# Linear attention beside a gated feed-forward block: x's statistics moved to the head of each iteration, and another order of loads where the token half changes

## The chip, the cores and the metric

The kernel runs on one core of a Trainium2 chip. A core has five engines, each with its own queue of instructions: PE (TensorE, matmuls), DVE (VectorE), ACT (ScalarE), POOL (GpSimd) and SP (SyncE), which here issues every DMA. The metric is the time on the device in microseconds (us), as the median of several runs. A trace comes from one more execution under the hardware profiler.

## What is computed

Everything is fp32. x has 2048 tokens of 576 values. It is normalized, and the result goes into two branches whose product is added to x:

```python
xn = layernorm(x)
q, k, v = split(xn @ wqkv)                    # 32 heads of 18
pq, pk  = phi(q), phi(k)                      # phi(t) = (t + 1 if t > 0 else exp(t)) + 1e-6
kv, z   = per head: pk^T v, sum of pk
s       = ((pq kv) / (pq z + 1e-6)) @ wo
g       = silu(gelu(xn @ w1 + b1) @ w2 + b2)  # w1: 576 x 4608, w2: 4608 x 576
out     = x + s * g
```

## The kernel before

A value is kept as two fp32r parts, high and low; a product is three matmuls (high by high, high by low, low by high). A "split" is a cast on ACT (high) and a subtraction on DVE (low).

**First stage** (the loop `for t in range(NT)`, 16 tiles of 128 tokens). Iteration t makes k and v of tile t and prepares later tiles. In program order: load of x of tile t+3; `project` for k (PE, 28 matmuls into pk); `transpose_x(t+1)` (five PE transposes of xn into pt, cast to xh on ACT, low part xl and a last block of xh on DVE); splits of w2's operand sums (`w2_hi`, `w2_lo`, tag w2o) and, in iterations 2 to 6, of w1's last rows (`we_hi`, `we_lo`, tag w1h); `layernorm(t+2)`; `phi` of k; `state(t-1)` (PE); `project` for v; `normalize_x(t+2)` (ACT writes xn); then on POOL the sums `w2_sum` and, in iterations 1 to 5, `we_sums`, and the addition of phi(k) to zacc; and the stores of what was split. `layernorm(t)` is two bn_stats, an aggregate and an add on DVE, the power -1/2 on POOL (`mv[:, 3:4]`), and for t of 2 and more a one-column product on DVE (L187, mean times -1/sqrt) that ACT uses as the bias in `normalize_x`. The instructions of each engine stand in the order of the program (`in_order`) until the end of the second stage. SP's DMAs are one queue; a DMA waits for the eighth before it.

The second stage makes q and the attention output. **The third stage** is the feed-forward block, 18 steps: the 9 chunks of w1 and w2 (512 hidden columns each), first over tokens 1024 to 2047 (half 0), then over the others (half 1). A step (base = 28 times its number) has an up part of two w1 tiles, n = 2 step and 2 step + 1, each seven products in the order UP = (1, 6, 7, 5, 2, 3, 4) of a Winograd scheme (L962, PSUM tiles a, b, zy, e), and a down part of seven products in the order ORDER = (1, 2, 7, 4, 5, 3, 6) (L1092, pm), whose results DVE adds to macc. PE, DVE, ACT and POOL follow program order; the extra work is put at places of the step by `add(base + place, function)`; places 0 to 13 follow the up products, 14 to 27 the down products. In half 0 the operands of w1 and w2 are made and stored; in half 1 they are loaded: `load_we` (we), `W1Loaded` (tiles a, c, d, and for odd n the tile e with operand 6 of both), `W2.load`.

The last step of half 0 is step 8 (NC is 9). In it the operands of x for half 1 are loaded over those of half 0: seven parts of 1 MiB (h0, l0, s2, h1, l1, s1, s4: high, low and sums of x's blocks, `load_x_part`) and, for each of the seven products, a last block of 128 rows (`load_rest`, two DMAs of 128 KB; into tiles rx for products 5, 2, 3, 4). `X_PARTS` says from where and into which place (`x_hi(b)` is xh of block b, `x_lo(b)` xl). In half 0 product 1 and 2 read xh2 and xl2, product 6 reads xh0, 5 xl1, 3 xl0, 7 and 4 xh3 and xl3. In half 1 product 1 and 2 read h0 and l0, 6 s2, 7 and 4 h1 and l1, 5 s1, 3 s4.

Of the kernel before, what the change touches and what calls it, by code (L numbers as in the profile page):

```python
# [42 lines left out]
def linear_attention_gated_ffn(ctx, tc, x, wqkv, wo, w1, w1e, b1, w2, b2, out):  # L43
# [36 lines left out]
    def bank2(name):  # L80
        return psum.tile([P, 2, 512], F32, tag="pp", name=name)
# [91 lines left out]
    def layernorm(t):  # L173
        st = t1.tile([P, 2, 6], F32, tag="st", name=f"st{t}")
        nc.vector.bn_stats(st[:, 0, :], xraw[t][:, :HD])
        nc.vector.bn_stats(st[:, 1, :], xraw[t][:, HD:])
        mv = t1.tile([P, 4], F32, tag="mv", name=f"mv{t}")
        nc.vector.bn_aggr(mv[:, 0:2], st)
        nc.vector.tensor_scalar_add(mv[:, 2:3], mv[:, 1:2], 1e-5)
        nc.gpsimd.tensor_tensor(mv[:, 3:4], mv[:, 2:3], nhalf, op=ALU.pow)  # L180
        xn[t] = t1.tile([P, 640], F32, tag="xn", name=f"xn{t}")
        if t < 2:
            for dst, src in norm_parts(t):
                nc.vector.tensor_scalar(dst, src, mv[:, 0:1], mv[:, 3:4], op0=SUB, op1=MUL)
        else:

            nc.vector.scalar_tensor_tensor(  # L187
                mv[:, 2:3], mv[:, 0:1], -1.0, mv[:, 3:4], op0=MUL, op1=MUL
            )
            stats[t] = mv  # L190

    def norm_parts(t):
        return (xn[t][:, :D], xraw[t]), (xn[t][:, D:], xraw[t][:, 512:])

    def normalize_x(t):
        mv = stats.pop(t)
        for dst, src in norm_parts(t):
            nc.scalar.activation(dst, src, AF.Identity, scale=mv[:, 3:4], bias=mv[:, 2:3])

# [230 lines left out]
    for t in range(NT):  # L430
        if t + 3 < NT:
            load_x(t + 3)
        if t == 1:
            we_load(0), we_load(1)
        pk = bank2(f"pk{t}")
        project(t, wk_h, wk_l, pk)
        if t == 0:
            for k in range(KT):
                split_w(raw_v[k], k, wv_h, wv_l, nc.vector)
        if t + 1 < NT:  # L440
            if t + 1 in (8, 12):
                x_block((t + 1) // 4)
            transpose_x(t + 1)
        for j in W2_SUMS.get(t - 1, ()):
            w2_hi(j)
        for j in W2_SUMS.get(t - 1, ()):
            w2_lo(j)
        if 2 <= t < 2 + WG:
            we_hi(t - 2), we_lo(t - 2)
        if t + 2 < NT:  # L450
            layernorm(t + 2)
        k_t, _ = phi(t1, pk, f"k{t}")
        if pend is not None:
            state(*pend)
        pv = bank2(f"pv{t}")
        project(t, wv_h, wv_l, pv)
        v_t = t1.tile([P, D], F32, tag="v", name=f"v{t}")
        nc.scalar.copy(as2(v_t), pv[:, :, :HD])
        if t + 2 < NT:
            normalize_x(t + 2)  # L460
        if t == 0:
            nc.gpsimd.memset(zacc, 0.0)
        for j in W2_SUMS.get(t, ()):
            w2_sum(j)
        if 1 <= t < 1 + WG:
            we_sums(t - 1)
        nc.gpsimd.tensor_tensor(zacc, zacc, k_t, op=ADD)
        for k in WQ_SPLITS.get(t, ()):
            split_w(raw_q[k], k, wq_h, wq_l, nc.gpsimd if k == 0 else nc.vector)
        for k in WQ_LOADS.get(t, ()):  # L470
            raw_q[k] = load_w_raw(0, k)
        for j in W2_SUMS.get(t - 1, ()):
            w2_store(j)
        if 2 <= t < 2 + WG:
            we_store(t - 2)
            if t < WG:
                we_load(t)
        for c in W2_LOADS.get(t, ()):
            w2_load(c)
        if t == KT + 2:  # L480
            make_mask()
            nc.gpsimd.memset(kvz, 0.0)
        pend = (t, k_t, v_t)
        if t in (4, 8):
            b = t // 4 - 1
            if b == 0:
                nc.sync.dma_start(x_dram[:, 0:4], xh[0][:, :4].bitcast(F32))
                nc.sync.dma_start(x_dram[:, 4:8], xl[0].bitcast(F32))
            else:
                nc.sync.dma_start(x_dram[:, 10:12], xh[1][:, 2:4].bitcast(F32))  # L490
                nc.sync.dma_start(x_dram[:, 14:16], xl[1][:, 2:].bitcast(F32))
# [164 lines left out]
        k, tag, bufs = (4, "w6", 1) if i == 6 else (8, "wa", 5)  # L656
        return w1p.tile([P, k, P], F32R, tag=tag, name=f"w{i}_{n}", bufs=bufs)

    we_sb = {}

    def load_we(n):

# [9 lines left out]
    class W1:  # L672
# [39 lines left out]
        def product(self, i):  # L712

            r = we_sb[self.n][:, WE_AT[i]]
            if i == 6:
                t = self.tiles[6]
                return t[:, :2], t[:, 2:], r
            key, k = {1: "a0", 2: "a1", 7: "c0", 3: "c1", 5: "d0", 4: "d1"}[i]
            t, k = self.tiles[key], 2 * int(k)
            return t[:, k : k + 2], t[:, 4 + k : 6 + k], r  # L720

    class W1Loaded(W1):


        def __init__(self, n):
            self.n, self.tiles = n, {}
            for i in ("a", "c", "d"):
                if n % 2 and i == "a":
                    t = w1_tile("e", n)
                    for k in range(2):  # L730
                        six = t[:, 4 * k : 4 * k + 4]
                        nc.sync.dma_start(six.bitcast(F32), w1_dram[(n - 1 + k) % NP, 6])
                        (w1t[n - 1] if k == 0 else self).tiles[6] = six
                if i == "c":
                    t = w1r.tile([P, 8, P], F32R, tag="stw", name=f"wc_{n}")
                else:
                    t = w1_tile(i, n)
                self.tiles[i] = t
                nc.sync.dma_start(t.bitcast(F32), w1_dram[n % NP, i])

    def spill(n):
        z = xsum[0]
# [493 lines left out]
    def x_operands(h0, l0, h1, l1, s1, s2, s4, rs):  # L1236
# [5 lines left out]
            3: (s4[:, A], s4[:, B]),  # L1242
        }.items()}

    X_PARTS = {
        "h0": (0, x_hi, 2, 1), "l0": (4, x_lo, 2, None), "s2": (16, x_hi, 0, 6),
        "h1": (8, x_hi, 3, 7), "l1": (12, x_lo, 3, None), "s1": (20, x_lo, 1, None),
        "s4": (24, x_lo, 0, None),
    }
    x_new = {}  # L1250

    def load_x_part(k):
# [64 lines left out]
    for step in range(n_chunks):  # L1317
# [4 lines left out]
        if half == 0:  # L1322
            plan_w1(add, w1t[2 * step + 1], base, **P1)
            add(base + 2, w2t[step].sum7)
            for i, at in PW2.items():
                add(base + at, w2t[step].hi, i)
                add(base + at + 1, w2t[step].lo, i)
            if step == 0:
                for i, at in W2_SUMS_FIRST.items():
                    add(at, w2t[0].load, i)  # L1330
        if not plain:
            add(base + 7, load_we, 2 * step + 2)
            add(base + 14, load_we, 2 * step + 3)
        if half == 0 and c < NC - 1:
            add(base + 0, make, W1, w1t, 2 * step + 2)
            add(base + 4, make, W1, w1t, 2 * step + 3)
            add(base + 1, lambda n=2 * step + 2, base=base: plan_w1(add, w1t[n], base, **P0))
            make(W2, w2t, step + 1)
            add(base + 22, w2t[step + 1].load_raw)
            for i, at in W2_SUMS_NEXT.items():  # L1340
                add(base + at, lambda i=i, n=step + 1: w2t[n].load(i))
        elif not plain:
            add(base + (14 if half == 0 else 7), make, W1Loaded, w1t, 2 * step + 2)
            add(base + 14, make, W1Loaded, w1t, 2 * step + 3)
            if step + 2 < n_chunks:
                make(W2, w2t, step + 1)
                for i, at in W2_NEXT.items():
                    add(base + at, lambda i=i, n=step + 1: w2t[n].load(i))
            else:
                make(W2, w2t, step + 1)  # L1350
                add(base + 7, w2t[step + 1].load_raw)
        if not plain:
            if half == 0 and c == NC - 1:
                for k, at in {"h0": 13, "l0": 13, "s2": 13, "h1": 15, "l1": 15, "s1": 15, "s4": 15}.items():
                    add(base + at, load_x_part, k)
                add(base + 15, lambda: x_new.update(rs=load_rests(0, (5, 2, 3, 4))))
                add(base + 25, silu_first, C11)
                for k in range(2):
                    add(base + 26 + k, combine, C12, nc.vector, slice(2 * k, 2 * k + 2))
                    add(base + 26 + k, combine, C21, nc.gpsimd, slice(2 * k, 2 * k + 2))  # L1360
            for what in ("S", "hi", "lo"):
                for (i, pr), at in PH[what].items():
                    add(base + at, getattr(h, what), i, pr)
        else:
            for f in range(CF):
                w2t[step].plain(f)
                add(base + (1, 2, 3, 8)[f], w2t[step].hi, ("p", f))
                add(base + (2, 3, 8, 9)[f], w2t[step].lo, ("p", f))
# [86 lines left out]
```

## Time and profile before

| what | us |
|---|---|
| median of 3 runs (lowest to highest) | 1121.29 (1120.52 to 1122.15) |
| the profiled execution | 1125.7 |
| its span, from first to last instruction | 1124.0 |
| PE busy in it | 1104.1 |
| DVE, ACT, POOL busy | 815.1, 455.9, 449.5 |

A row of a timeline is start, length, engine, line, operation, what is written from what is read, and in brackets the idle time of the engine before it and what ended that. A row of waits is who waited for whom: us in total, times, longest. A row of windows gives busy time and count by engine, then the clock that PE was granted (1.00 is full), the busy share of the DMA engines and GB/s. The chain is the work that ended last, followed back.

### The profile page before, as it was taken

The page shows a single profiled execution, that of the slowest core. Times are in us where ns is not written, and L with a number is a line of the kernel's source. Part 1 is how long each engine was busy: PE and PEld are TensorE (multiplying, and loading weights), DVE is VectorE, ACT ScalarE, POOL GpSimd, SP SyncE. Part 2 cuts the span into 40 slices and gives each one's busy share as a digit, 9 for nine tenths or more (in the row PEclk, how much of TensorE's full clock was granted, in tenths as well). Part 3 has the DMA queues.
Part 4 walks back from the last instruction along what each step waited for, and adds up shares of the span by engine and source line. Part 5 has one row for each costly group of instructions (what it writes and reads, how often), then busy time and mean ns, then how long its engine had stood idle before and what let it go on. Part 6 is the DMA issues. An engine that isn't in the chain of part 4 may idle for free.

```text
span 1124.0 us, 18604 instructions
## 1 busy us (share of the span) xinstructions
PE 1104.1 (98%) x6972; PEld 1019.6 (91%) x6972; DVE 815.1 (73%) x1159; ACT 455.9 (41%) x771; POOL 449.5 (40%) x392
## 2 busy tenths in 40 slices
PE   8989999999999999999999999899999999999997
PEld 8989998999998988989989889698998998989987
DVE  6776657989687787878877868376585674765856
ACT  4544444333544354454443534424233242232342
POOL 4666543333353452453534524225133242341340
PEclk9999999999999999999999999899999999999999
DMA  8698732364879559577595599996877786766552
GB/s 313 245 390 303 256 140 51 125 246 159 273 270 326 207 196 333 186 263 261 182 326 208 197 312 327 320 324 198 287 226 218 211 236 210 245 217 207 140 159 104
DMA packets 84969, 264.03 MB, mean 235 GB/s; under 512 B 10381, under 2 KB 20877, under 8 KB 81295
## 3 DMA queue, kind: packets, MB, share of 16 engines
q1 hardware_dynamic: 84879, 262.85, 68.8%
q8 instruction: 55, 0.90, 0.3%
q14 instruction: 35, 0.29, 0.1%
HBM read 166.69 MB, written 94.18 MB: 232 GB/s over the span
## 4 chain that ended last, share of the span: by engine, by line
PE 90%; DMA 5%; DVE 2%; issue 1%; SPq 0%; ACT 0%; POOL 0%; DVEq 0%; ACTq 0%; POOLq 0%
PE pm L1092 32%; PE a L962 10%; PE e L962 10%; PE zy L962 10%; PE pq L226 5%; PE b L962 5%; PE ps_s L625 5%; PE pv L226 4%; PE pk L226 4%; PE pd L1212 2%; DMA rx<-rq_dram 1%; DMA w1u<-w1e 1%; PE ps_kva L263 1%; DMA we<-we_dram 1%; DMA w__7651<-op 1%
## 5 line engine op out<-in xcount | busy, mean ns | idle before, releaser
L1099 DVE TENSOR_TENSOR macc<-pm,macc 128x576 f32<-128x576 f32 x218 | 164.4, 754 | 58.8 <-PE pm L1092 57.0
L649 ACT CAST h_h<-g 128x512 fp32r<-128x512 f32 x204 | 120.9, 620 | 135.9 <-PE pm L1092 134.7
L652 DVE TENSOR_TENSOR h_l<-g,h_h 128x512 fp32r<-128x512 f32 x204 | 164.8, 815 | 0.0
L1061 POOL TENSOR_TENSOR mid<-g 128x512 f32<-128x512 f32 x34 | 43.9, 1292 | 134.3 <-ACT g L970 134.3
L1055 POOL TENSOR_TENSOR g<-g 128x512 f32<-128x512 f32 x34 | 55.1, 1620 | 57.7 <-DVE h_l L652 56.4
L970 ACT ACTIVATE g<-b,b1c 128x512 f32<-128x512 f32 x36 | 24.8, 690 | 122.9 <-DVE b L988 122.9
L979 ACT COPY mid<-a 128x512 f32<-128x512 f32 x36 | 21.1, 587 | 117.4 <-PE a L962 117.4
L693 POOL TENSOR_TENSOR w1raw<-w1raw 128x256 f32<-128x256 f32 x18 | 16.9, 938 | 124.1 <-DVE wa L709 124.1
L982 DVE TENSOR_TENSOR mid<-b,mid 128x512 f32<-128x512 f32 x36 | 24.7, 687 | 44.9 <-PE b L962 43.2
L1058 POOL TENSOR_TENSOR g<-g 128x512 f32<-128x512 f32 x34 | 55.4, 1630 | 2.7
L1187 POOL TENSOR_TENSOR fin1l<-fin1h,fin1l 128x288 f32<-128x288 f32 x8 | 6.5, 807 | 121.9 <-DMA fin1l<-s_dram 56.6
L962 PE MATMUL a<-h0r,wa 128*128 128x512 f32 x144 | 51.5, 398 | 0.0
L988 DVE TENSOR_TENSOR b<-e,mid 128x512 f32<-128x512 f32 x36 | 25.2, 700 | 36.0 <-PE e L962 36.0
L962 PE MATMUL a<-xh,wa 128*128 128x512 f32 x144 | 50.6, 391 | 0.0
L1052 POOL TENSOR_TENSOR g<-g 128x512 f32<-128x512 f32 x34 | 46.7, 1373 | 2.7
L652 DVE TENSOR_TENSOR h_l<-mid,h_h 128x512 fp32r<-128x512 f32 x34 | 45.8, 1348 | 1.2
L590 POOL TENSOR_TENSOR pbuf<-phiq,den 128x576 f32<-128x576 f32 x16 | 20.4, 1276 | 63.6 <-DVE den L589 44.8
L985 DVE TENSOR_TENSOR mid<-zy,mid 128x512 f32<-128x512 f32 x36 | 24.9, 692 | 26.3 <-PE zy L962 26.3
L995 DVE TENSOR_TENSOR e<-e,mid 128x512 f32<-128x512 f32 x36 | 24.9, 691 | 22.8 <-PE e L962 22.7
L295 POOL TENSOR_TENSOR w2r<-w2r 128x576 f32<-128x576 f32 x27 | 41.0, 1526 | 0.7
L970 ACT ACTIVATE g<-e,b1c 128x512 f32<-128x512 f32 x36 | 24.9, 691 | 34.0 <-DVE e L995 33.9
L226 PE MATMUL pv<-wv_h,xh 128*128 128x288 f32 x160 | 35.5, 304 | 0.0
(810 smaller groups left out, 3611.8 us busy)
## 6 DMA issues: line engine op xcount, KB each, us to landing
we<-we_dram SPq DMA_DIRECT2D x72, 224.0 KB
op<-w2o SPq DMA_DIRECT2D x27, 576.0 KB
w2raw<-w SPq DMA_DIRECT2D x10, 1152.0 KB
w2r<-w SPq DMA_DIRECT2D x9, 1152.0 KB
w1raw<-w SPq DMA_DIRECT2D x18, 512.0 KB
op_a<-wa SPq DMA_DIRECT2D x18, 512.0 KB
op_c<-wc SPq DMA_DIRECT2D x18, 512.0 KB
op_d<-wd SPq DMA_DIRECT2D x18, 512.0 KB
```

Source lines behind the costliest of these rows:

```text
L226: nc.tensor.matmul(ps[:, h, :HD], st, w[:, k, h * HD : (h + 1) * HD], start=(i == 0), stop=(i == len(seq) - 1),)
L625: nc.tensor.matmul(ps[:, h, :HD], st[:, k, :], w[:, k, h * HD : (h + 1) * HD], start=(i == 0), stop=(i == len(seq) - 1),)
L649: nc.scalar.copy(pair[0], src)
L652: eng.tensor_tensor(pair[1], src, pair[0].bitcast(F32), op=SUB)
L962: nc.tensor.matmul(ps, st, mv, start=first and n == 0, stop=n == len(seq) - 1, skip_group_check=True,)
L970: nc.scalar.activation(g, ps, AF.Gelu_apprx_tanh, bias=b1c[:, f : f + 1])
L1052: tt(src[5, pr], A(1, 0), A(1, 1), op=ADD)
L1055: tt(src[6, pr], src[5, pr], A(0, 0), op=SUB)
L1058: tt(src[3, pr], A(0, 1), src[6, pr], op=SUB)
L1061: tt(src[7, pr], A(0, 0), A(1, 0), op=SUB)
L1092: nc.tensor.matmul(ps[:, q, :HD], hs[p][st][:, cs], m[:, p, :], start=(n == 0 and i not in CHAIN), stop=(n == len(seq) - 1), skip_group_ch ...
L1099: nc.vector.tensor_tensor(dst, src, dst, op=ADD)
```

## The change

In the first stage the statistics (bn_stats to power) of tile t+2 are issued at the head of iteration t, ahead of the projection, for t from 1; for t = 0 they stay behind the splits. The one-column product becomes a function of its own, `offset`, at the old place. The tile xn is taken where it is written.

In the last step of half 0 (`change`), x's parts get other places (h0 now into xh0, s2 into xh2, s1 into xl0, s4 into xl1) and other moments: h0 at 8, l0 and s2 at 11, h1, l1 and s1 at 13, s4 and the rests at 14. The first tile's weights are loaded at 11, the second's at 16, the w2 operands each ten places later. Operand 6 of both tiles is loaded by a function of its own, `load_six`, in half 1 at place 14 as before.

```diff
@@ layernorm and what follows it
         nc.gpsimd.tensor_tensor(mv[:, 3:4], mv[:, 2:3], nhalf, op=ALU.pow)
-        xn[t] = t1.tile([P, 640], F32, tag="xn", name=f"xn{t}")
+        stats[t] = mv
         if t < 2:
+            xn[t] = t1.tile([P, 640], F32, tag="xn", name=f"xn{t}")
...
-        else:
-
-            nc.vector.scalar_tensor_tensor(
-                mv[:, 2:3], mv[:, 0:1], -1.0, mv[:, 3:4], op0=MUL, op1=MUL
-            )
-            stats[t] = mv
+
+    def offset(t):
+
+        mv = stats[t]
+        nc.vector.scalar_tensor_tensor(
+            mv[:, 2:3], mv[:, 0:1], -1.0, mv[:, 3:4], op0=MUL, op1=MUL
+        )
...
         mv = stats.pop(t)
+        xn[t] = t1.tile([P, 640], F32, tag="xn", name=f"xn{t}")
@@ first stage, iteration t
+        if 0 < t < NT - 2:
+            layernorm(t + 2)
         pk = bank2(f"pk{t}")
...
+        if t == 0:
+            layernorm(2)
         if t + 2 < NT:
-            layernorm(t + 2)
+            offset(t + 2)
         k_t, _ = phi(t1, pk, f"k{t}")
@@ W1Loaded
-                if n % 2 and i == "a":
-                    t = w1_tile("e", n)
-                    for k in range(2):
-                        six = t[:, 4 * k : 4 * k + 4]
-                        nc.sync.dma_start(six.bitcast(F32), w1_dram[(n - 1 + k) % NP, 6])
-                        (w1t[n - 1] if k == 0 else self).tiles[6] = six
...
+    def load_six(n):
+
+        t = w1_tile("e", n)
+        for k in range(2):
+            six[n + k] = t[:, 4 * k : 4 * k + 4]
+            nc.sync.dma_start(six[n + k].bitcast(F32), w1_dram[(n + k) % NP, 6])
@@ x's parts
     X_PARTS = {
-        "h0": (0, x_hi, 2, 1), "l0": (4, x_lo, 2, None), "s2": (16, x_hi, 0, 6),
-        "h1": (8, x_hi, 3, 7), "l1": (12, x_lo, 3, None), "s1": (20, x_lo, 1, None),
-        "s4": (24, x_lo, 0, None),
+        "h0": (0, x_hi, 0, 1), "s4": (24, x_lo, 1, None), "l0": (4, x_lo, 2, None),
+        "s2": (16, x_hi, 2, 6), "s1": (20, x_lo, 0, None), "h1": (8, x_hi, 3, 7),
+        "l1": (12, x_lo, 3, None),
     }
+    X_AT = {"h0": 8, "l0": 11, "s2": 11, "h1": 13, "l1": 13, "s1": 13, "s4": 14}
@@ the plan of a step
+        change = step == NC - 1
         if not plain:
-            add(base + 7, load_we, 2 * step + 2)
-            add(base + 14, load_we, 2 * step + 3)
+            add(base + (11 if change else 7), load_we, 2 * step + 2)
+            add(base + (16 if change else 14), load_we, 2 * step + 3)
...
-            add(base + (14 if half == 0 else 7), make, W1Loaded, w1t, 2 * step + 2)
-            add(base + 14, make, W1Loaded, w1t, 2 * step + 3)
+            add(base + (11 if change else 7), make, W1Loaded, w1t, 2 * step + 2)
+            add(base + (11 if change else 14), load_six, 2 * step + 2)
+            add(base + (16 if change else 14), make, W1Loaded, w1t, 2 * step + 3)
...
-                    add(base + at, lambda i=i, n=step + 1: w2t[n].load(i))
+                    add(base + at + 10 * change, lambda i=i, n=step + 1: w2t[n].load(i))
...
-                for k, at in {"h0": 13, "l0": 13, "s2": 13, "h1": 15, "l1": 15, "s1": 15, "s4": 15}.items():
+                for k, at in X_AT.items():
                     add(base + at, load_x_part, k)
-                add(base + 15, lambda: x_new.update(rs=load_rests(0, (5, 2, 3, 4))))
+                add(base + 14, lambda: x_new.update(rs=load_rests(0, (5, 2, 3, 4))))
```

More of the change, by code (lines that the diff above doesn't have):

```diff
@@ L657, in w1_tile @@
         return w1p.tile([P, k, P], F32R, tag=tag, name=f"w{i}_{n}", bufs=bufs)
-    we_sb = {}
+    we_sb, six = {}, {}
     def load_we(n):
@@ L715, in product @@
             if i == 6:
-                t = self.tiles[6]
+                t = self.tiles[6] if self.n < NP else six[self.n]
                 return t[:, :2], t[:, 2:], r
```

## The prediction

> **What bounds the kernel now.** I read the page first: TensorE's line says that there is almost nothing to win anywhere but in its own gaps.
>
> ```profile
> PE   1104.1 (98%) x6972; PEld 1019.6 (91%) x6972; DVE 815.1 (73%) x1159; ACT 455.9 (41%) x771; POOL 449.5 (40%) x392
> ```
>
> So the second view is the one of who waited for whom, for PE alone. Two groups are larger than a microsecond in total and belong to the two stages that the diff touches: the transposes pt of the first stage, which wait for the normalized x (xn), and three operands at the change of token halves, which wait for their loads.
>
> ```profile
> PE pt L203 <- ACT xn L198: 4.4, 4, 1.1
> PE e L962 <- DMA rx<-rq_dram: 3.6, 1, 3.6
> PE e L962 <- DMA s1r<-x_dram: 1.0, 1, 1.0
> PE zy L962 <- DMA l1r<-x_dram: 0.9, 1, 0.9
> ```
>
> A stall costs more than its wait, so I take each stage's pace from the timeline and the chain. The rows are start, length, what. First stage:
>
> ```profile
> 39.56 0.77 PE L203 MATMUL pt<-ident,xn 128*128 128x128 f32 x5
> 49.96 0.77 PE L203 MATMUL pt<-ident,xn 128*128 128x128 f32 x5 [1.12 <-ACT xn L198]
> ...
> 81.03 0.77 PE L203 MATMUL pt<-ident,xn 128*128 128x128 f32 x5 [1.07 <-ACT xn L198]
> 82.80 3.77 PE pv L226 x28
> 91.86 3.77 PE pv L226 x28
> ```
>
> Four iterations, from the transpose of tile 4 (39.56) to that of tile 8 (81.03), take 41.47 us. An undisturbed one takes 91.86 - 82.80 = 9.06, four take 36.24. **The head loses 5.2 us.** Change of halves, from the chain:
>
> ```profile
> 588.36 22.55 PE pm L1092 x168
> 633.36 22.55 PE pm L1092 x168
> 732.23 22.55 PE pm L1092 x168
> ```
>
> A step takes 633.36 - 588.36 = 45.0; the two steps to 732.23 take 98.87 instead of 90.0. **The change of halves loses 8.9 us.** The three waits are 5.5 of it. Most of the rest is the clock:
>
> ```profile
> 713.11 0.77 PE L962 MATMUL e<-rx,we 128*128 128x512 f32 x1 [3.56 <-DMA rx<-rq_dram]
> ...
> 708.00:712.00 4.00, 1.55 (x6) 0.95 (x6) 0.00 (x0) 0.48 (x1) 0.00 (x0) 0.99 0.88 190
> 712.00:716.00 4.00, 2.89 (x7) 2.34 (x8) 0.70 (x1) 0.69 (x1) 0.00 (x0) 0.50 0.59 185
> 716.00:720.00 4.00, 4.00 (x14) 3.13 (x13) 0.56 (x1) 0.69 (x1) 0.00 (x0) 0.66 1.03 406
> ```
>
> The window rows end with granted clock, DMA share and GB/s. The clock is 0.50 from about 712 to 718.7: (0.01 + 0.50 + 0.34) x 4 = 3.4 us of clock lost, some 2.8 of them while there was work. PE had been idle only from 709.55 (713.11 - 3.56) when it fell.
>
> **The change, part by part: the head.** No instruction is added or removed; DVE's and POOL's counts are the same, and SP's order up to x8 is too. Moved are, per tile, two bn_stats, the aggregate and the add on DVE (and behind them the power on POOL) from after the splits of weights to the head of the iteration; the one-column product (offset, L187 before) stays. One old iteration, DVE and POOL, and two rows to compare:
>
> ```profile
> 72.20 0.69 DVE L212 TENSOR_TENSOR xl<-pt,xh 128x512 fp32r<-128x512 f32 x1 [1.32 <-ACT xh L211]
> 73.23 2.58 DVE L308 TENSOR_TENSOR w2o<-w2r,w2o 128x576 fp32r<-128x576 f32 x2
> 76.74 0.45 DVE L175 BATCH_NORM_STATS2 st<-x 128x6 f32<-128x288 f32 x1
> 77.83 0.15 DVE L179 TENSOR_SCALAR mv<-mv 128x1 f32<-128x1 f32 x1
> 78.71 1.37 DVE L187 SCALAR_TENSOR_TENSOR mv<-mv 128x1 f32<-128x1 f32 x1 [0.73 <-POOL mv L180]
> 80.48 0.76 DVE L236 SCALAR_TENSOR_TENSOR phik<-pk,ek 128x576 f32<-128x576 f32 x1
> ...
> 73.10 1.43 POOL L467 TENSOR_TENSOR zacc<-zacc,phik 128x576 f32<-128x576 f32 x1
> 78.13 0.55 POOL L180 TENSOR_TENSOR mv<-mv,nhalf 128x1 f32<-128x1 f32 x1 [3.60 <-DVE mv L179]
> 78.64 3.07 POOL L295 TENSOR_TENSOR w2r<-w2r 128x576 f32<-128x576 f32 x2
> ...
> 83.59 1.43 DVE L308 TENSOR_TENSOR w2o<-w2r,w2o 128x576 fp32r<-128x576 f32 x2
> 19.41 0.16 DVE L187 SCALAR_TENSOR_TENSOR mv<-mv 128x1 f32<-128x1 f32 x1 [0.73 <-POOL mv L180]
> ```
>
> From xl (72.20) to the next pt (81.03) run 8.83 us, and as pt also starts that round, this is what holds PE. Out of it go the statistics, 76.74 to 77.98 (1.24), and the wait for the power, 0.73: 6.86 are left. The offset needs 0.16 alone but 1.37 behind a POOL sum, the two splits 1.43 alone but 2.58 behind zacc (2.36 us of waiting behind POOL in all). POOL's sums now start earlier and meet the splits instead, so I keep those 2.36; without them 4.5 are left. PE needs 9.06 for the round, of which 1.5 lie between pt and xl (72.20 against 70.68 = 81.03 less one round of 10.35), so it may last 7.5: the four stalls go in either case. The transposes now take PSUM from phik, which ends 0.2 after the old pt (80.48 + 0.76 = 81.24); I count that inside the rounding.
>
> But **a wait is added**: the statistics of tile t+2 now stand on DVE ahead of xl of tile t+1, the splits, the offset and phi; behind them wait POOL's power and sums, ACT's xn, SP's stores, and PE. They need x one half iteration earlier. The late one is x8:
>
> ```profile
> 60.76 0.51 SPq L169 DMA_DIRECT2D x<-x  x1
> 64.81 8.10 DMA op<-w2o
> DMA packets 1290, 6.51 MB, mean 383 GB/s; under 512 B 143, under 2 KB 143, under 8 KB 903
> ```
>
> x8 is issued at 60.76; the store issued right behind it (576 KB) lands at 64.81 + 8.10 = 72.91, and at 383 GB/s it takes 1.5 of that: x8 lands between 71.4 and 72.9. I take 72.2, in a queue that is full and whose order does not change. Today its statistics start at 76.74 and wait for nothing; without the stalls they would be asked for at about 67. So xl of tile 7 starts at 72.2 + 1.24 = 73.5 instead of 72.20, and pt of tile 8 at 73.5 + 6.86 = 80.4 instead of 81.03. What the first three iterations win is given back at x8. **Head: 0.7 us saved**; bounds 0 (x8 at 72.9) and 3.0 (no waiting behind POOL). Later x tiles (x10, x12) have the same place but a full 9.06 round of PE to hide in; I cost them at nothing, and where that cover fails the slower rival below begins.
>
> **The change of halves.** The same loads in another order. At the old one, per SP's issues:
>
> ```profile
> 670.38 0.33 SPq L1255 DMA_DIRECT2D s2r<-x_dram  x1
> ...
> 679.26 1.18 SPq L668 DMA_DIRECT2D we<-we_dram  x2
> ...
> 689.21 0.32 SPq L1032 DMA_DIRECT2D w__7651<-op  x1
> 690.11 0.32 SPq L1255 DMA_DIRECT2D h1r<-x_dram  x1
> ...
> 696.35 16.54 SPq L809 DMA_DIRECT2D rx<-rq_dram  x8
> DMA packets 8351, 25.73 MB, mean 322 GB/s; under 512 B 899, under 2 KB 2947, under 8 KB 7444
> 700.75 0.40 PE L962 MATMUL a<-h0r,wa 128*128 128x512 f32 x1
> ```
>
> The queue is full from before 670 until 711, so what lands when is a matter of bytes ahead. In front of h1, l1, s1, s4 and the rests stand today the second tile's weights (we 0.46 MB, a, c, d 1.57 MB) and the first w2 operand (0.59 MB). The new order puts all 2.6 MB behind the rests. At 322 GB/s that is 8.1 us, at the 383 of the row above 6.8. rx of product 5 (landed 713.11) comes at 705.0 to 706.3; PE asks for it 27 matmuls after 700.75, at 0.23 each (1.61 for 7 in the chain's steady steps: 45.0 - 22.55 = 22.45 for 98), that is at 707.0. l1 and s1 move by the same and are asked for at 704.2 and 705.6: both in time, s4 too. No place comes free later than now: the first part loaded still waits for product 6 (670.4), and the part that took longest to get a place, h1, for the last product of the old half (678). So the three waits go, and with them the clock's fall: 8.9 us.
>
> What is late next is what was put behind: the second tile's a, asked for at 700.75 + 49 x 0.23 = 712.0. Between product 5's rx and its landing lie three rests (0.79 MB), we and a (0.98 MB): 1.77 MB, 5.5 us at 322: 710.5 to 711.8, plus the few tenths by which the last of 16 engines comes in behind the mean. I take 0.4 us of stall. The w2 operands (4.1 MB, four stores of 0.59 MB between them) follow the tile's c and d: the first lands at about 717 and is asked for at 723.4, the last at about 735 and is asked for six products of 3.2 later, at 742.7: covered. silu and combine on ACT and DVE lie beside the seven products, and today end while PE still waits for rx; at worst a gelu starts late, whose bank is asked for only products later. load_six and the renamed places cost nothing: the same DMAs in the same queue. **Change of halves: 8.9 - 0.4 = 8.5 saved.**
>
> **Sum.** 0.7 + 8.5 = 9.2. The profiled execution took 1125.7 (span 1124.0): it would take 1116.5. The median of the runs is 1121.29, 4.4 below, and no view says where those lie; PE's pace cannot give them, so part may be in the DMA stall, and then less can be won there. I subtract the full 9.2: **1112.1**.
>
> [...] In the new iteration 6 pk of tile 7 can go on only when xl is there (74.2), and 24 of its 28 matmuls at 3.77 for 28 take it to 77.4; pt follows at 80.4. PE idles 3.0 in one piece where it idled 1.07. At 709.55 to 713.11 above, the clock had fallen after some 2.4 of idling. [...]
>
> **Rivals.**
> 1. The clock falls in that gap: half of one to two spans like the one at 712 (3.4 us lost there) is 1.7 to 3.4. 1112.1 + 1.9 = 1114.0. For it: the row at 712. Against: the gaps of 1.1 did nothing, and less waiting behind POOL shrinks the gap. Chance 0.22.
> 2. x8 is early enough (by 69), or DVE gets through between POOL's sums: the head's whole 5.2 goes. 1121.3 - 8.5 - 5.2 = 1107.6. Against: the full queue. 0.10.
> 3. What was put behind comes too late: a of the second tile 2.5 us late instead of 0.4, and the clock falls again (2.8): 1112.1 + 2.1 + 2.8 = 1117.0. For: eight DMAs of 128 KB in a row, during which the rate above was 190 GB/s; at that rate the rests take 4.2 us instead of 2.5. 0.12.
> 4. Rivals 1 and 3 together: 1117.0 + 1.9 = 1118.9, about no change. 0.07.
> 5. Slower: DVE's wait at the head feeds itself. The stores of the splits are issued behind it, the next x stands behind these stores in SP's order, so x9 to x11 come late as well. At 2.8 us for each of x8 to x11, 11.2 us: 1121.3 - 8.5 + 11.2 = 1124.0. It decides from 8.5 / 4 = 2.1 us per tile. Against: after tile 8 POOL and DVE have less to do (no we sums, no we split). 0.07.
>
> **How the numbers follow.** My forecast has 0.42. Differences under 0.2% (2.2 us) are about what a measurement here cannot tell from none. Forecast and rivals 1 to 3 are faster by more: 0.86; rival 4 is within: 0.07; rival 5 slower: 0.07. The range goes from rival 2 to a little over rival 3, 1107.5 to 1118.0, and leaves out rivals 4 and 5. The 4.4 us between profile and median lie inside it.
>
> **What would show it.** Right: no PE wait for rx, s1r, l1r; clock 1.00 from 700 to 720; pt's waits for xn gone at tiles 5 to 7; a DVE wait of st for x some microseconds long at 67 to 72, and one PE gap of two to three ahead of the transpose of tile 8 at 80. Wrong: st never waits (rival 2); a clock below 1 near 80 (rival 1); PE waiting for wa or we near 712 (rival 3); several st waits (rival 5).

## The result, and the profile after

| | median us | lowest to highest | runs |
|---|---|---|---|
| before | 1121.29 | 1120.12 to 1122.94 | 5 |
| after | 1115.98 | 1114.33 to 1116.83 | 5 |

The ratio is 0.9951, with a 95% interval of 0.9936 to 0.9965: faster by 5.3 us where 9.2 were forecast. The predicted 1112.1 is 3.9 too low; the measured median lies inside the range of 1107.5 to 1118.0. The profiled execution of after took 1114.33 (span 1112.6), the best of its five; that of before took 1125.7, more than any of the five runs in the table. The two profiles therefore differ by 11.4 us and the medians by 5.3, and the first thing to explain is that gap.

First PE's line of the page of after, then who PE waited for, the groups that concern the two stages:

```profile
PE 1100.2 (99%) x6972; PEld 1018.2 (92%) x6972; DVE 806.6 (72%) x1159; ACT 454.8 (41%) x771; POOL 455.1 (41%) x392
```

```profile
PE pt L206 <- ACT xn L201: 2.2, 1, 2.2
...
PE pk L229 <- ACT v L465: 0.8, 1, 0.8
```

The three operands of the change of halves are gone from the list, and of the four waits of the transposes one is left, longer than each of them was. The wait of pk is new: it stands at 73.29, in the same round as the one that is left, so PE loses 3.0 us there in two pieces. (The profile puts it down to the copy of v out of PSUM. Every execution with the long wait has these 0.8, none without it does, and no run here shows more of its cause.) The next fence is the timeline of after around that wait: DVE, then PE's transposes (start, length, what).

```profile
64.33 0.76 DVE L239 SCALAR_TENSOR_TENSOR phik<-pk,ek 128x576 f32<-128x576 f32 x1
71.61 0.46 DVE L175 BATCH_NORM_STATS2 st<-x 128x6 f32<-128x288 f32 x1 [6.52 <-DMA x<-x]
72.71 0.15 DVE L179 TENSOR_SCALAR mv<-mv 128x1 f32<-128x1 f32 x1
72.78 0.68 DVE L215 TENSOR_TENSOR xl<-pt,xh 128x512 fp32r<-128x512 f32 x1
73.82 3.66 DVE L311 TENSOR_TENSOR w2o<-w2r,w2o 128x576 fp32r<-128x576 f32 x2
...
48.93 0.71 PE L206 MATMUL pt<-ident,xn 128*128 128x128 f32 x5
57.98 0.71 PE L206 MATMUL pt<-ident,xn 128*128 128x128 f32 x5
67.03 0.71 PE L206 MATMUL pt<-ident,xn 128*128 128x128 f32 x5
79.51 0.77 PE L206 MATMUL pt<-ident,xn 128*128 128x128 f32 x5 [2.22 <-ACT xn L201]
```

Tiles 5, 6 and 7 come at a round of 9.05 without a wait. Then DVE stands still for 6.52 us with the statistics of tile 8 at its head, because x8 has not landed. xl of tile 7, ready to run behind them, starts at 72.78; the splits of w2o take 3.66 where they took 2.58 before, with POOL's sums of w2r beside them (73.52 to 76.86); and the transpose of tile 8 starts 7.9 us after x8 landed. The chain of waits of after puts the landing in the same place (start, length, what; 59.46 + 12.13 = 71.59), and further down shows the third stage:

```profile
59.46 12.13 DMA x<-x
...
586.54 22.55 PE pm L1100 x168
631.54 22.55 PE pm L1100 x168
676.54 22.55 PE pm L1100 x168
721.54 22.55 PE pm L1100 x168
```

Every step takes 45.0, that across the change too. Step 6 (the 588.36 of before) starts at 586.54. The windows of after at the change of halves (PE, PEld, DVE, ACT, POOL, then granted clock, DMA share, GB/s):

```profile
700.00:704.00 4.00, 4.00 (x20) 3.27 (x19) 4.00 (x4) 2.74 (x3) 2.29 (x2) 1.00 0.70 194
704.00:708.00 4.00, 4.00 (x19) 3.29 (x18) 1.47 (x3) 3.72 (x4) 0.00 (x0) 1.00 0.96 309
```

PE is full and the clock is 1.00 here, and so to 720. So in this pair of executions the change of halves gives its whole 8.9, the head 588.36 - 586.54 = 1.8, and the rest, about 0.7 of 11.4, lies elsewhere.

### The profile page after: what moved, and what is told of

It reads as the page before. It is cut to its first block, busy times and chain, and to the rows that moved or that the text cites. A ratio compares the mean times of both kernels' runs of the same rounds, so it can differ in the third digit from the quotient of the medians.

```text
span 1112.6 us, 18603 instructions
## 1 busy us (share of the span) xinstructions
PE 1100.2 (99%) x6972; PEld 1018.2 (92%) x6972; DVE 806.6 (72%) x1159; ACT 454.8 (41%) x771; POOL 455.1 (41%) x392
## 4 chain that ended last, share of the span: by engine, by line
PE 94%; DVE 2%; DMA 2%; POOL 1%; issue 1%; ACT 0%; SPq 0%; DVEq 0%; ACTq 0%
PE pm L1100 34%; PE a L970 10%; PE e L970 10%; PE zy L970 10%; PE b L970 5%; PE pq L229 5%; PE ps_s L632 5%; PE pv L229 4%; PE pk L229 4%; PE pd L1220 2%; DMA x<-x 1%; PE ps_kva L266 1%; PE ptp L614 1%; PE pt L206 1%; PE ps_kw L560 1%
## 5 line engine op out<-in xcount | busy, mean ns | idle before, releaser
L229 PE MATMUL pk<-wk_h,xh 128*128 128x288 f32 x160 | 34.5, 297 | 1.5 <-ACT v L465 0.8
```

The lines of the kernel that those rows point to most:

```text
L229: nc.tensor.matmul(ps[:, h, :HD], st, w[:, k, h * HD : (h + 1) * HD], start=(i == 0), stop=(i == len(seq) - 1),)
```

## The experiments

Two things are open. Why is the median's gain 5.3 if one pair of executions shows all the forecast steps? **Theory A:** the stall at the change of halves varies from run to run, the profiled execution of before had a bad one, and the usual stall is about 5. **Theory B:** the stall is as large as the profile said, and something in after takes the gain back in most runs. And is x8's place in the full queue (376 GB/s from 55 to 80 us in after) really what holds the head, or would the head stall anyway? All times of a group are against runs of before on the same chip: a median of 1121.69 (24 runs, 1119.43 to 1126.36) for the first four kernels, 1123.38 (20 runs, 1119.83 to 1127.01) for the last four.

### The kernel before again

No edit.

> The kernel before once more, unchanged, for the spans and granted clocks of its usual runs. The predicted sum was 9.2 us, the profiled pair differs by 11.4, the medians by 5.3. Theory A (the profiled execution of before was one of its worse ones: the clock fell in its stall at the change of halves, in the usual run it does not, or the stall is shorter): spans of 1118.5 to 1121, clocks nearer 1.00 than 0.996, and a profile whose two steps across the change take 94 to 96 us instead of 98.9. Theory B (before always loses 14 us, and the changed kernel's usual run loses to a clock fall in the new gap what its profiled run did not): clocks of 0.996 in every run of before, and a profile as the first one, 1125.7 us.

Measured: median 1121.5 (12 runs, 1119.75 to 1128.12), ratio 1.0001 (0.9985 to 1.0017). The profiled execution took 1123.07. Its waits, its chain and its windows, the counterparts of those in the prediction:

```profile
PE pt L203 <- ACT xn L198: 4.4, 4, 1.1
PE e L962 <- DMA rx<-rq_dram: 3.0, 1, 3.0
```

```profile
588.61 22.55 PE pm L1092 x168
633.61 22.55 PE pm L1092 x168
...
729.60 22.55 PE pm L1092 x168
```

```profile
708.00:712.00 4.00, 1.73 (x4) 1.47 (x5) 0.70 (x1) 0.92 (x2) 0.00 (x0) 0.69 0.67 150
712.00:716.00 4.00, 4.00 (x11) 3.03 (x11) 0.00 (x0) 1.19 (x2) 0.00 (x0) 0.50 1.00 409
```

The same kernel, the same place, another size: one wait of 3.0 instead of three of 5.5 together, and two steps of 729.60 - 633.61 = 95.99: 6.0 lost, not 8.9. The head's row is the same to a tenth. Theory A was wrong on the clock, though: the mean granted clocks of the twelve runs are 0.993 to 0.999, eight of them 0.997, about what a profiled execution with one fall of 3.4 us shows below (0.997 or 0.998). So a usual run of before seems to have a fall as well, and it is the size that varies. The stall at the change of halves is a matter of when DMAs land; the head's is not.

### The head alone

The first-stage hunks of the change on the kernel before; the third stage is that of before.

```diff
+        if 0 < t < NT - 2:
+            layernorm(t + 2)
         pk = bank2(f"pk{t}")
...
         if t + 2 < NT:
-            layernorm(t + 2)
+            offset(t + 2)
```

> Only the edits of the first stage (statistics at the head of the iteration, offset, xn's tile); the change of halves as before. My theory (x8's landing sets the transpose of tile 8): that transpose at 79.5 as in the changed kernel instead of 81.0, 1.5 us saved, 1119.8; up to 1.7 more if the clock falls in the gap, 1121.5. Rival (the whole head stall goes, and the measured 5.3 is all from the head): 1116.1.

Measured: median 1121.2 (12 runs, 1117.92 to 1123.93), ratio 0.9995 (0.9983 to 1.0007). By itself this half can't be told from no change. Its waits show why it isn't worth the 1.8 that the profile of after had, together with its windows:

```profile
PE pt L206 <- ACT xn L201: 2.5, 1, 2.5
```

```profile
76.00:80.00 4.00, 1.47 (x11) 1.23 (x11) 3.96 (x6) 1.19 (x2) 1.08 (x1) 0.98 0.74 306
80.00:84.00 4.00, 4.00 (x23) 4.00 (x22) 3.25 (x8) 2.39 (x5) 3.91 (x4) 0.59 1.02 331
```

PE idles 2.5 us ahead of pt of tile 8, and right behind it the clock is 0.50 for 3.4 us: rival 1, which took place here and not in the profiled execution of after. Its chain:

```profile
588.67 22.55 PE pm L1099 x168
633.67 22.55 PE pm L1099 x168
...
728.34 22.55 PE pm L1099 x168
```

Step 6 starts at 588.67, no earlier than before (588.36 and 588.61). The other runs fit a fall that comes in some executions only: of the twelve, the five with a mean clock of 0.995 or 0.996 took 1121.27 to 1123.93 us; of the seven with 0.997 or 0.998, six took 1117.92 to 1121.12 and one 1122.40. And the change of halves, untouched here, lost 728.34 - 633.67 - 90.0 = 4.7. PE's wait for rx ends there at 710.21, and the clock falls behind it:

```profile
711.00:712.00 1.00, 1.00 (x5) 0.76 (x4) 0.42 (x1) 0.54 (x1) 0.00 (x0) 0.67 0.85 169
```

### The change of halves alone

The third-stage hunks of the change (X_PARTS, X_AT, load_six, the moments) on the kernel before; the head is that of before.

> Only the edits of the third stage (places, moments and order of the loads, load_six); the first stage as before. My theory: the step across the change takes 45.0 us and no PE wait for rx, s1r or l1r is left; by the profiles that is 8.9, 1112.4; by the medians (5.3 less the head's 1.5) 3.8, 1117.5. Rival (the change of halves gives nothing, the loads being bound by the queue): 1121.3.

Measured: median 1116.82 (7 runs, 1116.35 to 1118.46), ratio 0.9958 (0.9944 to 0.9973). In its profiled execution all steps take 45.0:

```profile
633.59 22.55 PE pm L1093 x168
678.59 22.55 PE pm L1093 x168
723.59 22.55 PE pm L1093 x168
```

So the stall goes completely, and its going is worth 1121.69 - 1116.82 = 4.9 between medians (3.0 to 6.3 by the ratio's interval). The two halves add up: 0.5 + 4.9 against 5.3 for both. Of the 11.4 between the two profiles, the medians therefore keep 4.9 of the stall's 8.9, as theory A says, and 0.5 of the head's 1.8. This second, smaller part is theory B's: in some executions a fall of the clock in the new gap takes the head's gain back.

### x one iteration earlier

Kernel after, but each x tile is loaded one iteration sooner, so that x8 stands in the queue where x7 stood. No instruction is added.

```diff
     load_x(2)
+    load_x(3)
...
-        if t + 3 < NT:
-            load_x(t + 3)
+        if t + 4 < NT:
+            load_x(t + 4)
```

> The changed kernel with every x tile from 3 on loaded one iteration earlier (load_x of tile t+4 at the head of iteration t), so that x8 stands where x7 stood. My theory (x8's place in a full queue holds DVE): x8 lands at 57 instead of 71.6, the transpose of tile 8 comes near 76 instead of 79.5, no st waits for x, no gap at 80, 3.5 us saved and with the gap any clock fall there: 1112.5 and less spread between runs. Rival (DVE's waits behind POOL set the pace of the head once x is there): the transpose of tile 8 at 78 to 79, 1115.0.

Measured: median 1111.92 (6 runs, 1111.10 to 1114.88), ratio 0.9914 (0.9897 to 0.9932). DVE's timeline in the place where it stood still for 6.52:

```profile
64.88 0.45 DVE L175 BATCH_NORM_STATS2 st<-x 128x6 f32<-128x288 f32 x1
...
68.39 0.69 DVE L215 TENSOR_TENSOR xl<-pt,xh 128x512 fp32r<-128x512 f32 x1 [2.27 <-ACT xh L214]
```

The statistics wait for nothing, no wait of pt for ACT's xn is left, and the transpose of tile 8 comes at 75.96, where 76 was expected. What is new stands 690 us later, in PE's waits:

```profile
PE pm L1101 <- DVE h_l L660: 1.8, 1, 1.8
...
PE a L971 <- DMA wa<-op_a: 0.5, 1, 0.5
```

The second is the second tile's a (wa), 0.5 late, about the 0.4 that the prediction gave it; in after it was in time. The two steps across the change take 90.8 here instead of 90.0. The first is new: in step 10 POOL stands in program order at the sums of an output tile, whose operands are late. The groups of POOL's waits:

```profile
POOL fin1l L1196 <- DMA fin1l<-s_dram: 72.7, 4, 28.9
```

Behind it POOL's sums for h come late, then ACT, DVE (h_l) and PE. This execution, with 1114.88, was the worst of the six. The smaller spread that was expected did not come: these runs lie 3.8 apart, those of after 2.5.

### The order of the loads alone, the places alone

"Places" here means the new places and the new moments of x's parts. Both kernels are after with one part of its third stage put back. In the first, x's parts have their old places and moments and only the weights and w2 operands come later:

```diff
     X_PARTS = {
-        "h0": (0, x_hi, 0, 1), "s4": (24, x_lo, 1, None), "l0": (4, x_lo, 2, None),
-        "s2": (16, x_hi, 2, 6), "s1": (20, x_lo, 0, None), "h1": (8, x_hi, 3, 7),
-        "l1": (12, x_lo, 3, None),
+        "h0": (0, x_hi, 2, 1), "l0": (4, x_lo, 2, None), "s2": (16, x_hi, 0, 6),
+        "h1": (8, x_hi, 3, 7), "l1": (12, x_lo, 3, None), "s1": (20, x_lo, 1, None),
+        "s4": (24, x_lo, 0, None),
     }
-    X_AT = {"h0": 8, "l0": 11, "s2": 11, "h1": 13, "l1": 13, "s1": 13, "s4": 14}
+    X_AT = {"h0": 13, "l0": 13, "s2": 13, "h1": 15, "l1": 15, "s1": 15, "s4": 15}
...
-                add(base + 14, lambda: x_new.update(rs=load_rests(0, (5, 2, 3, 4))))
+                add(base + 15, lambda: x_new.update(rs=load_rests(0, (5, 2, 3, 4))))
```

> The kernel after with x's parts back at their old places and moments (h0, l0, s2 at 13, the others and the rests at 15), but the weights of both tiles and the w2 operands at their new moments: the order of the loads alone. Theory (bytes ahead in a full queue decide): the 2.6 MB that stood in front of the rests are behind them, but x's parts start at place 13 instead of 8, 1.6 us a place, so up to 8 us of the queue is used less. Most of the about 5 us of the change of halves is saved, rx of product 5 on the edge (wait 0 to 1.5 us): median 1116.5 to 1118.5. Rival (the places that come free first decide): the gain is under half of that, 1119.5 to 1121, and PE still waits for rx about 3 us.

Measured: median 1117.3 (9 runs, 1114.09 to 1121.37), ratio 0.995 (0.9933 to 0.9968). PE waits for no operand at the change in its profiled execution; the steps across it take 45.0. (In step 10 PE waits 0.4 for h_l, the place where the kernel with the early x waited 1.8.)

In the second, the weights and w2 operands have their old moments:

```diff
-        change = step == NC - 1
+        change = False
```

> The kernel after with x's parts at their new places and moments, but the weights of both tiles and the w2 operands at their old moments (7, 14 and 15 on): the places alone. Theory (bytes ahead decide): s4 and the rests stand behind both tiles' weights as they did, so PE still waits for rx 1.5 to 3 us, the waits for l1r and s1r are gone: median 1117.5 to 1119.5. Rival (the places decide): PE waits for no rest, about 1116.

Measured: median 1118.39 (12 runs, 1115.95 to 1122.41), ratio 0.9962 (0.9947 to 0.9977). Its waits and chain:

```profile
PE e L970 <- DMA rx<-rq_dram: 2.3, 1, 2.3
```

```profile
631.75 22.55 PE pm L1100 x168
724.25 22.54 PE pm L1100 x168
```

The wait for rx is still there, 2.3, and the two steps lose 92.50 - 90.0 = 2.5, but the clock stays at 1.00. This execution (1116.9) is one of the better ones: the six runs of this kernel below its median have mean clocks of 0.998 or 0.999, the six above it 0.996 or 0.997. This is what the theory of bytes ahead in a full queue (322 GB/s from 655 to 735 us in before) asked for in both: the order alone clears the stall in the profiled execution, the places alone leave the rests behind the weights. In SP's issues the last of x's parts, s4, comes at 685.93 in after, at 688.75 with the order alone (whose steps start 1.8 later, 588.35 against 586.54) and at 695.50 with the places alone, where s1 still goes ahead of the second tile's weights (we) and s4 stands behind them. First the order alone, then the places alone:

```profile
688.75 0.32 SPq L1265 DMA_DIRECT2D s4r<-x_dram  x1
689.46 14.71 SPq L817 DMA_DIRECT2D rx<-rq_dram  x8
```

```profile
680.65 0.33 SPq L1265 DMA_DIRECT2D s1r<-x_dram  x1
684.11 1.14 SPq L675 DMA_DIRECT2D we<-we_dram  x2
...
695.50 0.32 SPq L1265 DMA_DIRECT2D s4r<-x_dram  x1
696.59 10.81 SPq L817 DMA_DIRECT2D rx<-rq_dram  x8
```

The medians, 1.1 apart with wide runs, do not separate the two; neither is told from after by its ratio. The rows tell them apart.

These two have the head of after unchanged, so each has its gap too, ahead of pt at 79.7. Windows of the order alone, then of the places alone:

```profile
80.00:84.00 4.00, 4.00 (x23) 4.00 (x22) 3.54 (x8) 2.39 (x5) 3.91 (x4) 0.57 1.01 330
```

```profile
80.00:84.00 4.00, 4.00 (x35) 4.00 (x34) 3.72 (x8) 2.39 (x4) 3.92 (x4) 1.00 1.01 322
```

The clock fell in one and not in the other.

### The head alone, with x early

The head alone from above with each x tile one iteration sooner; the third stage is that of before. It tells whether x8's place is all that kept the head from its 5.2.

> The kernel before with the statistics at the head (the first-stage part of the change) and each x tile loaded one iteration earlier, the third stage as before. Theory (x8's place in the full queue is all that kept the head from its 5.2 us): no wait of pt for xn in the head but the first, no clock below 1 near 80, and the step of pm that starts at 318.6 starts at 313; the change of halves as before. Median 1121.6 - 5.2 = 1116.4, range 1115.5 to 1117.5. Rival (the gain of the early x comes only together with the new order at the change of halves): 1119 to 1121.

Measured: median 1116.12 (6 runs, 1115.29 to 1117.27), ratio 0.9941 (0.9925 to 0.9957). The forecast median was 1116.4. That it was met so closely is partly luck: the forecast started from 1121.6, and before stood at 1123.38 on this chip; by the ratio the gain is 6.6, not 5.2. Windows and chain:

```profile
76.00:80.00 4.00, 4.00 (x35) 4.00 (x33) 2.85 (x6) 2.39 (x4) 1.87 (x2) 1.00 1.03 430
80.00:84.00 4.00, 4.00 (x33) 4.00 (x32) 1.85 (x5) 1.73 (x3) 2.93 (x7) 1.00 1.02 365
```

```profile
582.58 22.55 PE pm L1100 x168
627.58 22.55 PE pm L1100 x168
722.23 22.55 PE pm L1100 x168
```

Step 6 starts at 582.58 instead of 588.36 or 588.61: the head's whole stall is gone, 5.8 to 6.0 (the 5.2 was counted from tile 4 to tile 8 alone). The step of pm that was expected at 313 starts at 312.56. The change of halves loses its 722.23 - 627.58 - 90.0 = 4.65, as in the head alone (4.7).

### x early, and POOL's sums out of step 10

Kernel after with the early x, and output tile 8's sums moved from step 10 into steps 11 and 12, one half tile in each, into places of h that are free there.

```diff
-        if half == 1 and 1 <= c <= 8:
-            for k in range(2):
+        if half == 1 and 2 <= c <= 8:
+            jobs = [(7 + c, 0, 0), (7 + c, 1, 1)]
+            if c <= 3:
+                jobs.append((8, c - 2, 2))
+            for t, k, at in jobs:
```

> The kernel with the early x loads (x of tile t+4 at the head of iteration t) in which the sums of output tile 8, which POOL made in step 10, are made in steps 11 and 12, one half of the tile in each, so that POOL has nothing to wait for in step 10. Theory (POOL stands in step 10 behind loads of the last rest of the queue's backlog; h of step 10 comes late in some runs): no PE wait for h_l near 766, every step after the change 45.0 us, runs from 1111.0 to 1112, median 1111.2 (0.7 less than with POOL's sums in step 10), and the spread of the runs (1111.1 to 1114.9) is smaller. Rival (that run was slow for another reason, the clock or the DMA rate): median 1111.9 and the same spread; or the third load in steps 11 and 12 makes the same wait there.

Measured: median 1111.16 (6 runs, 1110.84 to 1112.05), ratio 0.9898 (0.9881 to 0.9915). This is the fastest of these kernels. In PE's waits nothing over 0.6 is left beside the first one, 1.6 for the identity; each step takes 45.0, and POOL takes up step 10 six microseconds earlier than with the early x alone (753.12 against 759.18). Its timeline, then that of the early x alone:

```profile
753.12 1.29 POOL L1070 TENSOR_TENSOR mid<-g 128x512 f32<-128x512 f32 x1 [27.39 <-ACT g L979]
```

```profile
755.67 0.81 POOL L1196 TENSOR_TENSOR fin1l<-fin1h,fin1l 128x288 f32<-128x288 f32 x1 [28.95 <-DMA fin1l<-s_dram]
...
759.18 1.29 POOL L1070 TENSOR_TENSOR mid<-g 128x512 f32<-128x512 f32 x1
```

That the wait is gone is shown. That it was worth 0.8 in the median isn't: the two ratios' intervals overlap, and the kernels ran on different chips.

## Why the prediction was right or wrong, step by step

The stall at the change of halves, in five profiled executions with the old order of loads or part of it (two steps without a stall take 90.0; the clock's time at 0.50 from windows of 1 us):

| kernel | two steps | lost | PE waited there | clock at 0.50 |
|---|---|---|---|---|
| before | 98.87 | 8.9 | 5.5 | 6.8 |
| before again | 95.99 | 6.0 | 3.0 | 6.8 |
| head alone | 94.67 | 4.7 | 2.8 | 3.4 |
| head alone, x early | 94.65 | 4.65 | 2.8 | 3.4 |
| places alone | 92.50 | 2.5 | 2.3 | 0 |

**"The change of halves loses 8.9 us": the term that was mis-sized.** The mechanism was right: the waits, the clock's fall and their going together came as forecast. But 8.9 is the largest of the four executions that have the old loads whole, and a typical one loses 4.7 to 6.0; between medians the term is 4.9. The prediction saw that the profiled execution stood 4.4 above the median, wrote that part of this may lie in the DMA stall, and then subtracted the full 9.2 from the median. 8.9 less 4.4 is 4.5: almost all of the excess would lie in this stall and in the clock that falls with it, and before again bears that out: it took 2.6 less than the first profiled execution, and its stall was 2.9 smaller. With 4.9 in place of 8.9 - 0.4 the sum would have been 1121.29 - 0.7 - 4.9 = 1115.7, against 1115.98. That the other term, the head's 0.7, comes so close to the 0.5 of the medians is luck: by the rows it is 1.5 to 1.8 or nothing, as told below.

**The second tile's a, 0.4 late:** 0 in after, 0.5 with the early x. The size is right, its sum is not. The rests were given 322 GB/s; the window of after from 696 to 700, in which they land, shows 202, near the 190 of rival 3. But product 5's rx had landed by 701.3, when SP had issued the second we, the eighth DMA behind it (SP waits for the landing eight places back: in after 3.3 us for s4, 2.0 for s1 and 1.5 for l1, each ahead of an rx); that is 2 us ahead of the earliest time forecast (705.0, less the head's 1.8). The two errors work against each other. Rival 3 (2.5 late and another fall) was in no trace.

**The order of bytes.** Right as a cause, with one correction. The prediction gave the whole saving to the 2.6 MB of weights that move behind the rests and costed the renamed places at nothing. The new places and moments of x's parts alone reduced the stall to 2.5 in their profiled execution. There h1, l1 and s1 are issued from 676.55 to 680.65, ahead of the second tile's we (684.11), where before issues them from 690.11 on, behind it (679.26). The first part itself comes no earlier: 668.77 against 670.38 is the 1.6 by which these steps start sooner. By the profiles either half of the edit takes away most of the stall, so their gains do not add; by the medians the two kernels cannot be told from after.

**The head: x8 holds it.** Right, and its numbers came close: x8 landed at 71.59 (bounds 71.4 to 72.9, taken 72.2), 7.9 us to pt (8.1 taken: 1.24 and 6.86), pt at 79.51 (80.4; the 0.7 follows from 80.3, the same terms unrounded). Of the 2.36 of waiting behind POOL that were kept, 2.23 reappear at the splits (3.66 against 1.43). The saving at that row is 1.5 instead of 0.7, mainly because x8 was 0.6 early. Rival 2 did not take place in after, but the early x made its condition true: then the head's whole stall goes, and the median with both stages is 1111.9.

**Rival 1, the clock in the new gap, took place in some executions.** Four profiled executions have the same head and a gap of 2.2 to 2.5 us in the same place: the clock stayed at 1.00 in after (gap 2.22) and the places alone (2.54), and fell in the head alone (2.53) and the order alone (2.29). Step 6 starts at 586.54 and 586.75 without a fall, at 588.67 and 588.35 with one: 1.6 to 2.1 us, what rival 1 gave it (1.9), and just what the head had saved. So the head is worth 1.8 or nothing, execution by execution; in the medians, 0.5 with an interval that reaches past nothing. It was wrong to treat the fall as a case that holds for all runs or for none. Of the five runs of after, the four slower ones (spans 1114.1 to 1115.1 against 1112.6) are not all explained in this way. The mean clock takes in the last few us, where it is lower (0.69 from 1120 to 1124 in before, 0.95 from 1110 on in after). The profiled executions without a fall ahead of that have a mean of 0.999 or 1.000, those with one of 3.4 us 0.997 or 0.998; of these four runs two have 0.997, but two have 0.999. What made the last two 1.7 and 2.5 us longer stays open.

**The length of the gap does not decide alone.** Falls followed gaps of 1.76 (the early x, step 10), 2.29 (the order alone), 2.53, 2.82, 2.84, 2.95 and 3.56 us, while gaps of 2.22, 2.29 (the places alone, at the change) and 2.54 did nothing. The forecast weighed the new gap by the fall at 712, after some 2.4 of idling; gaps both shorter and longer than that did nothing. What else decides, no run here shows.

**Rival 5** (DVE's wait feeds itself) did not take place: after x8, the statistics of tile 9 start at 79.63 with no wait. Those of tiles 10 and 12 do wait, 1.04 and 1.28 in after, and PE waits for neither of them: the round hides them, as forecast.

## What to carry to other kernels

A profiled execution that stands above the median has its excess somewhere; here most of it lay in what varies, a DMA stall and the clock that falls with it (8.9 and 6.0 us in two executions of before). Size such a term by what the median can hold, not by that one execution. When work with an input from a DMA is put at the head of an in-order engine, look for the one input that lands latest and move its load too; here two lines of loads, added to the reorder of the statistics, were worth far more than the reorder by itself (a ratio of 0.9941 against 0.9995). The early loads without the reorder were not run; in before the statistics of tile 8 wait for no load. And four short stalls made into one long one are not the same stall: in before the four, of 1.1 us each, left the clock at 1.00; the one of 2.2 to 2.5 us cost a fall of 3.4 us in two executions of four.

## What was not expected of the hardware

- **The falls had two lengths.** In each of these falls the clock was 0.50 for 3.4 us or for 6.8; 3.4 us at 0.50 are 1.7 us of full-speed work. The longer falls came at the change of halves in the two executions whose wait was longest in one piece (3.56 and 2.95 us); there PE still idled 1.2 and 0.7 us after the clock had fallen, elsewhere it did not. The second 3.4 us are most of the difference between a loss of 4.7 and one of 6.0.
- **The fall can come after the idle time is over.** In the head alone the gap ends at 79.73 and the clock falls at about 79.86; in the order alone it ends at 79.72 and the clock falls at about 80.16. The longest delay is at the change of halves of the head alone: the gap ends at 710.21, and the clock falls at about 711.34, with PE busy. What sets the delay, no run here shows.
- **The same loads land at other times.** POOL's first sum of the output tile in step 10, which waits for its load, started at 753.03 in after and at 755.67 with the early x, though step 10 came 2.8 us sooner there. In the one it cost PE nothing, in the other 1.8 us and a fall of the clock behind it (0.71 in the window from 768).
